# Column-tile key-value blocks for batches 2 and 3, with the second gate difference ahead of their scalings

## The chip, the cores and the metric

The kernel runs on one core of a Trainium2 chip. The metric is the device time of one execution in microseconds (us); less is better. Most executions agree within 0.3%. Times of one comparison come from the same chip and the same rounds.

## The reference, cut to what matters

```python
# attention without a score matrix, 8 batches, 8 heads, 576 tokens, 64 per head
q_s = softmax(q, axis=-1)                    # over the 64 of a head
k_s = softmax(k, axis=2)                     # over the tokens
kv  = einsum('bhsd,bhse->bhde', k_s, v)      # a 64x64 matrix per head
x   = einsum('bhsd,bhde->bhse', q_s, kv)     # -> (4608, 512)
# then a two-layer network
h = x @ w_in                                 # 512 -> 2048
g = h / (1 + exp(-beta * h))
out = g @ w_out                              # 2048 -> 512
```

## The kernel before

The work goes in nine slabs of 512 tokens. In slab t, TensorE makes the hidden tiles (`XT,WIN` matmuls, L387), ScalarE applies the gate, VectorE scales, and then (from slab 1 on) an output stage runs 112 gate products (L754) by a seven-product scheme that needs sums and differences of the gate halves. Attention for the next batches is fitted into the output stage. All engines run their own instructions in the order in which the program lists them. `tick` counts TensorE's progress; a pair `(99, f)` means that f is listed when the count reaches 99.

What the change touches:

```python
def tiled(b):
    return b > 3

# key-value products, one pair of heads: full 128-column matmul, or two
# 64-column matmuls side by side on two column tiles
if not tiled(b):
    mm(PS[bk][:, 256*n:256*n + VW-1], l, r_[:, 0:VW-1], j == 0, j == 4, ...)
for h in range(2) if tiled(b) else ():
    e.matmul(PS[bk][64*h:64*h+64, ...D+1], l[:, p], r_[:, HW*h:HW*h+D+1],
             tile_position=(0, 64*h), ...)
# when a pair of head pairs is done, VectorE scales it into weights ("scaling")
e.reciprocal(RC...)                           # L461
kvd(b, h2, bk, 256*m)                         # L433: KVD <- PS, RC, MASK
...
def g_diff(fh):                               # gate difference, L720, VectorE
    # GT[half] -= GT[other half], 128x2048 bf16, both inputs in SBUF

def norm_turn(b, hp0):                        # queries of two head pairs
    norm_main(b, hp0, 2, POOL)                # sums on VectorE, scaling on GpSimd (L343)
    turn(b, hp0, 2)                           # transpose by DMA: QT <- EQ

def attn_late(b):
    ...                                       # x: the four query products QT,KVD
    if b < 4:
        s = spread(kv_steps(b, (0, 1)), 97, 101) + spread(kv_steps(b, (2, 3)), 101, 105)
        s += [(105, lambda: g_diff(1))]
        return s + spread(x[0:2], 117, 120)
    s = [(96, steps(kv_all, b)), (99, lambda: g_diff(1))]
    return s + spread(x, 107, 123)
...
# slabs 1 and 2, output stage
on(2, norm_turn, 2, 0)
on(3, norm_turn, 2, 2)
on(3, g_diff, 0)
```

A query product has the scaled keys (KVD) as weights and the transposed queries (QT) as data, so it needs both.

The softmax here doesn't subtract the row's maximum and nothing guards it: scores larger than these inputs give would overflow.

Of the kernel before, what the change touches and what calls it, by code (L numbers as in the profile page):

```python
# [42 lines left out]
class Program:  # L43
# [12 lines left out]
    def add(self, eng, fn, r=(), w=(), bank=(), slot=None, after=(), war=False):  # L56
        op = Op(eng, fn, slot)
        op.pos = len(self.ops)
        deps = op.deps
        deps.extend(after)  # L60
        for k in r:
            deps.extend(self.writer.get(k, ()))
            self.readers.setdefault(k, []).append(op)
        for k in w:
            for d in self.readers.get(k, ()):
                if d is not op and (war or not self._same(d, op)):
                    deps.append(d)
            for d in self.writer.get(k, ()):
                if not self._same(d, op):
                    deps.append(d)  # L70
            self.readers[k] = []
            self.writer[k] = [op]
        for k in bank:
            t = self.touch.setdefault(k, {})
            for e, d in t.items():
                if e != eng:
                    deps.append(d)
            t[eng] = op
        if eng == POOL and slot is None:
            if self.pool is not None:  # L80
                deps.append(self.pool)
            self.pool = op
        self.ops.append(op)
        return op
# [71 lines left out]
def bass_efficient_attn_shen__then__act_swish_beta_kernel(  # L156
# [12 lines left out]
    with ExitStack() as es:  # L169
# [209 lines left out]
        def bank(pool=MB):  # L379
            rot[0] += 1  # L380
            return pool[rot[0] % len(pool)]

        def mm(o, l, r_, start, stop, r=(), w=(), bk=0, tr=False):
            if tr:
                add(PE, lambda e: e.transpose(o, l, r_), r=r, w=w, bank=[bk])
            else:
                add(PE, lambda e: e.matmul(o, l, r_, start=start, stop=stop), r=r, w=w, bank=[bk])  # L387
# [22 lines left out]
        def kv_rows(b, hp, j):  # L410
            i = b % 2
            pi = (b // 2) % 2
            if j < 4:
                return (bass.AP(EK[i], hp * 512 + j * 128, [[2048, 128], [1, 128]]),
                        VB[i][:, j, hp, :], [("ek", i, hp)], [("vb", i, hp)], [("vone", i)])
            if b < 2:
                return (bass.AP(EKS[b], hp * 128, [[512, 128], [1, 128]]), VRS[b][:, hp, :],
                        [EKSK[b]], [("vrs", b)],
                        [("vrs0", b), ("vrsone", b, 0), ("vrsone", b, 1)])
            return (bass.AP(EKR[pi], hp * 128, [[512, 128], [1, 128]]),  # L420
                    VR[pi][b % 2][:, hp, :], [("ekr", pi, 0), ("ekr", pi, 1)],
                    [("vr", pi, b % 2)], [("vr0", pi, b % 2), ("vrone", pi, b % 2)])
# [2 lines left out]
            return b if b < 2 else 2 + b % 4  # L425

        def tiled(b):
            return b > 3

        def kvd(b, hp, bk, c):  # L430
            i = b % 2
            a = bass.AP(PS[bk], c, [[512, 128], [0 if tiled(b) else HW, 2], [1, D]])
            add(DVE, lambda e: e.scalar_tensor_tensor(  # L433
                KVD[kd(b)][:, hp, :].rearrange("p (a b) -> p a b", b=D), a, RC[i][:, hp:hp + 1],
                MASK[:, :].rearrange("p (a b) -> p a b", b=D), ALU.mult, ALU.mult),
                r=[("ps", bk), ("rc", i, hp), "mask0", "mask1", "mask2"], w=[("kvd", kd(b), hp)],
                bank=[bk])

        def kv_steps(b, hps, pool=MB):
            i = b % 2  # L440
            st = {}

            def one(n, hp, j):
                if n == 0 and j == 0:
                    st["b"] = bank(pool)
                bk = st["b"]
                l, r_, ke, kv, ko = kv_rows(b, hp, j)
                if not tiled(b):
                    mm(PS[bk][:, 256 * n:256 * n + VW - 1], l, r_[:, 0:VW - 1], j == 0, j == 4,
                       r=ke + kv, w=[("ps", bk)], bk=bk)  # L450
                for h in range(2) if tiled(b) else ():
                    p = slice(64 * h, 64 * h + 64)
                    add(PE, lambda e, h=h, p=p: e.matmul(  # L453
                        PS[bk][p, 256 * n:256 * n + D + 1], l[:, p], r_[:, HW * h:HW * h + D + 1],
                        start=j == 0, stop=j == 4, tile_position=(0, 64 * h),
                        skip_group_check=True),
                        r=ke + kv, w=[("ps", bk)], bank=[bk])
                if n == len(hps) - 1 and j == 4:
                    c, k_ = hps[0], len(hps)
                    s_ = bass.AP(PS[bk], D, [[512, 128], [256, k_]])  # L460
                    add(DVE, lambda e: e.reciprocal(RC[i][:, c:c + k_], s_),  # L461
                        r=[("ps", bk)], w=[("rc", i, h2) for h2 in hps], bank=[bk])
                    for m, h2 in enumerate(hps):
                        kvd(b, h2, bk, 256 * m)
            return [lambda n=n, hp=hp, j=j: one(n, hp, j) for n, hp in enumerate(hps)
                    for j in range(5)]
# [6 lines left out]
        def out_step(b, hp, pool=MB, eng=DVE):  # L473
            i = b % 2

            def one():
                bk = bank(pool)
                out_mm(b, hp, bk)
                add(eng, lambda e: (e.copy if eng == ACTE else e.tensor_copy)(  # L479
                    XT[i][:, hp, :], PS[bk][:, :]),  # L480
                    r=[("ps", bk)], w=[("xt", i, hp)], bank=[bk])
            return [one]
# [43 lines left out]
        def steps(fn, *a):  # L526
            return lambda: go(fn(*a))
# [12 lines left out]
        def attn_late(b):  # L540
            x = []
            for hp in range(NHP):
                x += out_step(b, hp, MB, ACTE if hp % 2 else DVE)
            if b < 4:
                s = spread(kv_steps(b, (0, 1)), 97, 101) + spread(kv_steps(b, (2, 3)), 101, 105)
                s += [(105, lambda: g_diff(1))]
                return s + spread(x[0:2], 117, 120)
            s = [(96, steps(kv_all, b)), (99, lambda: g_diff(1))]
            return s + spread(x, 107, 123)

        def spread(steps, lo, hi):
            return [(lo + (hi - lo) * k / len(steps), s) for k, s in enumerate(steps)]
# [8 lines left out]
        def go(steps):  # L561
            for s in steps:
                s()
# [137 lines left out]
        def gv(f, th, n):  # L701
            return GT[:, f:f + n, 256 * th:256 * th + 256]

        def gk(f, th, n):
            return [("gt", f + x, th) for x in range(n)]
# [12 lines left out]
        def g_diff(fh):  # L718
            f, th = NG * fh, 1 - fh
            add(DVE, lambda e: e.tensor_tensor(gv(f, th, NG), gv(f, th, NG), gv(f, 1 - th, NG),  # L720
                                               ALU.subtract),
                r=gk(f, 0, NG) + gk(f, 1, NG), w=gk(f, th, NG), war=True)
# [140 lines left out]
        for t in range(NSLAB):  # L863
# [135 lines left out]
            elif t + 2 < B:  # L999
                b = t + 2  # L1000
# [46 lines left out]
```

## Time and profile before

| | before |
|---|---|
| time, median of 3 runs | 273.48 us |
| span in the profile | 271.7 us |
| TensorE busy | 97% |
| VectorE busy | 71% |

The page gives the share of each engine and "the chain that ended last", which follows the end of the program back through what released each step. The timeline lists instructions as start, duration, engine, line, operation, output and inputs. DVE is VectorE, ACT ScalarE, POOL GpSimd, PE TensorE's matmuls and PEld its weight loads.

### The profile page before, as it was taken

To read this page: it belongs to the slowest core of one execution; us is meant where nothing else is said; L and a number is where in the kernel's file an instruction comes from. 1 tells how busy PE (TensorE), PEld (TensorE's weight loads), DVE (VectorE), ACT (ScalarE), POOL (GpSimd) and SP (SyncE) were. 2 spreads that over 40 slices of the span, in tenths; PEclk is the share of its full clock that TensorE was granted. 3 is DMA by queue.
4 is the path that set the end of the run, shared out by engine and by line. 5 is a ranking of instruction groups with operands and counts; after the bars stand their busy time and mean duration, and the time that the engine had idled before them with its cause. 6 is when DMAs were issued, how large, how long until landed. Compare 5 with 4: busy or idle time off the path is not lost.

```text
span 271.7 us, 4811 instructions
## 1 busy us (share of the span) xinstructions
PE 263.8 (97%) x1882; PEld 165.7 (61%) x1905; DVE 194.0 (71%) x416; ACT 181.0 (67%) x284; POOL 64.1 (24%) x80
## 2 busy tenths in 40 slices
PE   8899999999999999999999999999999999999994
PEld 3444444448844885478646865687458745874683
DVE  4964586887867799878786977787687548626762
ACT  4898558789287956897778847893883387018610
POOL 2790010006530089000910870037000100000000
PEclk9999999999999999999999999999999999999999
DMA  7999999989799129930499999203800130012005
GB/s 220 314 201 207 227 321 349 303 227 373 173 337 285 65 53 299 332 95 2 89 282 283 308 345 182 103 20 65 208 0 2 31 142 2 0 69 88 0 5 152
DMA packets 59366, 45.93 MB, mean 169 GB/s; under 512 B 28608, under 2 KB 58320, under 8 KB 58320
## 3 DMA queue, kind: packets, MB, share of 16 engines
q1 hardware_dynamic: 54480, 40.90, 53.4%
q0 software_dynamic: 4240, 4.19, 9.4%
q10 hardware_dynamic: 624, 0.53, 0.6%
q8 instruction: 15, 0.25, 0.4%
q14 instruction: 7, 0.06, 0.1%
HBM read 36.71 MB, written 9.44 MB: 170 GB/s over the span
## 4 chain that ended last, share of the span: by engine, by line
PE 85%; DVE 4%; DMA 4%; POOL 2%; SPq 2%; issue 2%; ACT 1%; POOLq 0%
PE PS L387 51%; PE PS L754 33%; DMA VF<-in_v_dram 2%; DMA QT<-EQ 1%; PE PS L453 1%; POOL VB L358 1%; SPq L275 1%; DVE QS L339 1%; SPq L287 1%; DVE EQ L343 1%; POOL EQ L343 1%; DVE VB L358 1%; ACT GT L654 1%; POOL VR L372 0%; DVE QI L341 0%
## 5 line engine op out<-in xcount | busy, mean ns | idle before, releaser
L387 PE MATMUL PS<-XT,WIN 128*128 128x512 bf16 x562 | 126.2, 379 | 1.1 <-issue 0.3
L654 ACT ACTIVATE GT<-PS,BETA 128x512 bf16<-128x512 f32 x144 | 95.1, 689 | 37.8 <-PE PS L387 37.5
L387 PEld LDWEIGHTS PS<-XT,WIN 128*128 128x128 bf16 x576 | 55.2, 98 | 64.4 <-DVE XT L479 0.6
L677 DVE TENSOR_SCALAR GT<-GT,RB 128x512 bf16<-128x512 bf16 x144 | 52.1, 382 | 36.5 <-ACT GT L654 35.6
L343 POOL TENSOR_TENSOR EQ<-EQ,QI 128x1024 bf16<-128x1024 bf16 (+1 forms) x13 | 25.6, 1967 | 46.9 <-DVE QI L341 46.3
L754 PE MATMUL PS<-WOUT,GT 128*128 128x256 bf16 x256 | 33.0, 273 | 0.1
L754 PE MATMUL PS<-WOUT,GS 128*128 128x256 bf16 x256 | 31.9, 273 | 0.2
L754 PE MATMUL PS<-WSUM,GT 128*128 128x256 bf16 x256 | 30.4, 273 | 0.5 <-DMA QT<-EQ 0.4
L754 PEld LDWEIGHTS PS<-WSUM,GT 128*128 128x128 bf16 x256 | 25.0, 98 | 3.8 <-issue 0.3
L754 PEld LDWEIGHTS PS<-WOUT,GT 128*128 128x128 bf16 x256 | 24.9, 98 | 3.5
L790 ACT COPY O2S<-PS 128x512 f32<-128x512 f32 (+1 forms) x17 | 9.4, 560 | 25.6 <-PE PS L754 24.2
L754 PEld LDWEIGHTS PS<-WOUT,GS 128*128 128x128 bf16 x256 | 24.1, 98 | 3.4
L307 ACT ACTIVATE EQ<-QF 128x512 bf16<-128x512 f32 x32 | 17.9, 620 | 7.3 <-DMA QF<-in_q_dram 7.2
L358 POOL CAST VB<-VF 128x512 bf16<-128x512 f32 x24 | 16.7, 694 | 23.0 <-DVE GS L713 14.1
L713 DVE TENSOR_TENSOR GS<-GT 128x512 bf16<-128x512 bf16 (+2 forms) x32 | 21.9, 685 | 0.0
L339 DVE TENSOR_REDUCE QS<-EQ 128x16 f32<-128x1024 bf16 (+1 forms) x20 | 19.8, 991 | 0.9 <-ACT EQ L307 0.9
L720 DVE TENSOR_TENSOR GT<-GT 128x2048 bf16<-128x2048 bf16 x16 | 20.1, 1281 | 0.0
L307 ACT ACTIVATE EK<-KF 128x512 bf16<-128x512 f32 x32 | 18.1, 620 | 0.1
L479 ACT CAST XT<-PS 128x512 bf16<-128x512 f32 x18 | 10.3, 581 | 10.7 <-PE PS L387 10.7
L802 DVE TENSOR_TENSOR O2S<-TS,PS 128x512 f32<-128x512 f32 (+1 forms) x17 | 10.7, 643 | 9.5 <-PE PS L754 9.5
L754 PE MATMUL PS<-WSUM,GS 128*128 128x256 bf16 x128 | 16.7, 273 | 0.0
L387 PE MATMUL PS<-WOUT,GT 128*128 128x512 bf16 x62 | 15.0, 379 | 0.1
(82 smaller groups left out, 225.5 us busy)
## 6 DMA issues: line engine op xcount, KB each, us to landing
out_dram<-O2S SPq DMA_DIRECT2D x8, 1024.0 KB, 5.4
QF<-in_q_dram SPq DMA_DIRECT2D x6, 1024.0 KB, 5.9
KF<-in_k_dram SPq DMA_DIRECT2D x6, 1024.0 KB, 8.5
VF<-in_v_dram SPq DMA_DIRECT2D x6, 1024.0 KB, 12.2
KF<-in_k_dram SPq DMA_DIRECT2D x8, 256.0 KB, 5.5
VF<-in_v_dram SPq DMA_DIRECT2D x8, 256.0 KB, 5.5
WOUT<-in_moe_w_out_dram POOLq DMA_DIRECT2D x4, 512.0 KB, 16.4
WIN<-in_moe_w_in_dram POOLq DMA_DIRECT2D x3, 512.0 KB, 9.0
```

Source lines behind the costliest of these rows:

```text
L307: add(ACTE, lambda e, o=o, a=a: e.activation(o, a, ACT.Exp), r=[(name + "f", i, hp)], w=[("e" + name, i, hp)])
L339: add(DVE, lambda e: e.tensor_reduce(s_, a, AX.X, ALU.add), r=ks, w=[("qs", i, hp0)])
L343: add(eng, lambda e: e.tensor_tensor(a, a, vb, ALU.mult), r=ks + [("qi", i, hp0)], w=ks)
L358: add(eng, lambda e: (e.copy if eng == ACTE else e.tensor_copy)(o, a), r=[("vf", i, hp), ("vone", i)], w=[("vb", i, hp)], after=after)
L387: add(PE, lambda e: e.matmul(o, l, r_, start=start, stop=stop), r=r, w=w, bank=[bk])
L479: add(eng, lambda e: (e.copy if eng == ACTE else e.tensor_copy)(XT[i][:, hp, :], PS[bk][:, :]), r=[("ps", bk)], w=[("xt", i, hp)], bank=[bk])
L654: add(ACTE, lambda e: e.activation(GT[:, f, :], PS[bk][:, :], ACT.Silu, scale=BETA[:, f:f + 1]), r=[("ps", bk), "beta"], w=[("gt", f, 0), ...
L677: add(DVE, lambda e: e.tensor_scalar(GT[:, f, :], GT[:, f, :], RB[:, f:f + 1], None, ALU.mult), r=k + ["rb"], w=k)
L713: add(DVE, lambda e: e.tensor_tensor(GS2[:, i:i + n, :], GT[:, i:i + n, :], GT[:, i + NG:i + NG + n, :], ALU.add), r=[k_ for f in (i, i + ...
L720: add(DVE, lambda e: e.tensor_tensor(gv(f, th, NG), gv(f, th, NG), gv(f, 1 - th, NG), ALU.subtract), r=gk(f, 0, NG) + gk(f, 1, NG), w=gk(f ...
L754: add(PE, lambda e, l=l, r_=r_, st=st, u=u, i=i, b_=b_: e.matmul(PS[b_][:, 256 * u:256 * u + 256], l, r_, start=st, stop=end and i == NG - ...
L802: add(DVE, lambda e, b_=b_, u0=u0, u1=u1: e.tensor_tensor(o[:, u0:u1, :], ts[:, u0:u1, :], bank3(b_)[:, u0:u1, :], ALU.add), r=["ts", ("ps ...
```

## The change

The intent: batches 4 to 7 already have their key-value products as blocks on column tiles, which take TensorE less time (0.84 us for a batch, measured in slab 3, against an estimated 1.13); batches 2 and 3 get them too. With the block in one piece, the second gate difference is put ahead of the block in the program, and so ahead of its scalings on VectorE.

```diff
         def tiled(b):
-            return b > 3
+            return b > 1
...
             if b < 4:
-                s = spread(kv_steps(b, (0, 1)), 97, 101) + spread(kv_steps(b, (2, 3)), 101, 105)
-                s += [(105, lambda: g_diff(1))]
+                s = [(99, lambda: g_diff(1)), (101, steps(kv_all, b))]
                 return s + spread(x[0:2], 117, 120)
```

## The prediction

> **What bounds the kernel now.** I read first the page's busy shares and the chain that ended last, then the timeline of the two places that the change touches, then the waits there, then a later stage for the rule that decides.
>
> ```profile
> PE 263.8 (97%) x1882; PEld 165.7 (61%) x1905; DVE 194.0 (71%) x416; ACT 181.0 (67%) x284; POOL 64.1 (24%) x80
> ...
> PE 85%; DVE 4%; DMA 4%; POOL 2%; SPq 2%; issue 2%; ACT 1%; POOLq 0%
> ```
>
> TensorE carries 85% of the chain. A TensorE saving therefore counts, unless TensorE runs into a wait right behind it. The change touches only the output stages of slabs 1 and 2 (the key-value products of batches 2 and 3), so I look there. The chain in order of time, slab 1:
>
> ```profile
> 66.96 1.91 POOL EQ L343
> 68.86 0.02 issue
> 68.88 3.53 DMA QT<-EQ
> 72.41 0.27 issue
> 72.68 0.49 PE PS L754 x3
> ```
>
> Here TensorE does not set the time. The query scaling on GpSimd and its transpose DMA do: TensorE stands before the first query product until 72.45, when the transpose lands. The timelines of VectorE, then of GpSimd, at that place (start, duration):
>
> ```profile
> 68.68 1.26 DVE L720 TENSOR_TENSOR GT<-GT 128x2048 bf16<-128x2048 bf16 x1
> 69.86 0.16 DVE L461 RECIPROCAL RC<-PS 128x2 f32<-128x2 f32 x1
> 70.05 0.61 DVE L433 SCALAR_TENSOR_TENSOR KVD<-PS,RC,MASK 128x128 bf16<-128x128 f32 x2
> 70.58 0.16 DVE L461 RECIPROCAL RC<-PS 128x2 f32<-128x2 f32 x1
> 70.77 0.61 DVE L433 SCALAR_TENSOR_TENSOR KVD<-PS,RC,MASK 128x128 bf16<-128x128 f32 x2
> 71.30 1.48 DVE L720 TENSOR_TENSOR GT<-GT 128x2048 bf16<-128x2048 bf16 x1
> 72.88 0.69 DVE L479 CAST XT<-PS 128x512 bf16<-128x512 f32 x1
> ```
> ```profile
> 68.94 2.76 POOL L343 TENSOR_TENSOR EQ<-EQ,QI 128x1024 bf16<-128x1024 bf16 x1
> ```
>
> L720 is a gate difference, L461 and L433 are the key-value scalings. GpSimd's second query scaling takes 2.76 us beside the first gate difference, its twin just before took 1.91. And the second gate difference, begun at 71.30, ends 1.08 us after GpSimd's end at 71.70. In slab 2 the same rows stand at 97.25 (first difference), 97.50 (GpSimd, 2.76) and 99.86 (second difference, end 101.34). The waits from 94 to 106 us, slab 2:
>
> ```profile
> PEld PS L387 <- DMA QT<-EQ: 0.5, 2, 0.3
> PEld PS L754 <- issue: 0.3, 1, 0.3
> ```
>
> The two QT waits are for the first and the second transpose. The "issue" one ends at 101.46, just after the second gate difference: it is the wait for it.
>
> **What the Trainium skill says.** "SBUF — State Buffer", section "Who interferes with whom": VectorE and GpSimd share a port pair, an exclusive lock for the whole instruction; a VectorE operation with two SBUF inputs contends with a GpSimd operation that reads SBUF. The trace agrees: gate differences are such operations, and the 2.76 and 1.48 above are these locks. "VectorE: DVE Perf Modes", section "The perf-mode tier table", gives 1224 ns for a bf16 tensor_tensor of 2048 elements; the undisturbed ones in this trace take 1218 ns. "TensorEngine Tiling (Array Packing)", section "Key Properties", says that changing the tiling mode drains TensorE; the gap of some 0.1 us at the end of the tiled block below agrees. "TensorE: Matmul & The Clock Gate", section "What's actually happening", puts the idle window before a slower clock at some 3.4 us; no wait here shows it, and the ones that I predict are shorter.
>
> What happens when VectorE issues two contending instructions in a row while GpSimd waits? Slab 4 shows it:
>
> ```profile
> 152.91 2.77 DVE L720 TENSOR_TENSOR GT<-GT 128x2048 bf16<-128x2048 bf16 x2
> 152.94 1.66 POOL L358 CAST VB<-VF 128x512 bf16<-128x512 f32 x1
> ...
> 154.04 1.63 DVE L720 TENSOR_TENSOR GT<-GT 128x2048 bf16<-128x2048 bf16 x1
> ```
>
> The cast (0.61 us when alone) waits out the first difference, which ends at 154.12, and ends at 154.60; the second difference, issued at 154.04, then takes until 155.67, 1.07 us after the cast. So they alternate: the waiting GpSimd goes in between the two.
>
> **The change part by part.**
>
> (a) TensorE. Per batch, 20 full matmuls of 131 columns, strewn among gate products, become 40 matmuls of 65 columns in one block, pairs side by side on two column tiles. Before: from one gate product to the next takes 0.11 us, with a key-value matmul between 0.167, so about 0.057 each and 20 x 0.057 = 1.13 us. After, from batch 4 in slab 3, already tiled: the block begins at 123.80 (0.11 after the gate product before it at 123.69), the next gate product at 124.64: 0.84 us. Saved: 0.29 us per batch. The block also starts 7 gate products later (0.76 us), so the wait for the key exponentials (0.22 us at 67.69, slab 1) vanishes. TensorE reaches the first query product of slab 1 some 0.5 us earlier, of slab 2 0.3 us earlier. But it waits there already for the transpose, which the change does not speed up: all of this is lost in a longer wait.
>
> (b) VectorE. No work is removed. The order first difference, scalings, second difference becomes first difference, second difference, scalings. By the alternation of slab 4 the second difference, though issued at 69.86 in slab 1, waits until GpSimd ends at 71.70 and ends at 72.77: the very time at which it ended before. GpSimd and the transposes do not move. What moves is the four scalings. They ran in the shadow of the GpSimd operation (69.86 to 71.38); they now begin after 72.77. From the end of a gate difference (69.93) to the end of the first scaling (70.40) took 0.47 us, to the last (71.38) 1.45 us. So the first scaling ends at 72.77 + 0.47 = 73.24 in slab 1 and 101.34 + 0.47 = 101.81 in slab 2.
>
> (c) The path. The first query product has the scaled keys as weights. From VectorE's end to TensorE's start I take 0.12 us (second difference end 101.34, weights at 101.46).
> Slab 1: 73.36 instead of 72.45: +0.91. Behind it, the next query product needs the second scaling at 73.50, and arrives there at 73.8; the second transpose landed by 74.97 and is wanted at 75.9; the cast of the first query output goes from 73.88 at most to 74.8, wanted at 75.9. No further wait: +0.91 stays.
> Slab 2: 101.93 instead of 100.58: +1.35. The wait for the second difference is gone; in matmul starts it cost 101.49 - 101.36 = 0.14. The wait for the second transpose (103.53 against 103.45 without it: 0.08) goes too, as TensorE now comes later than the landing. The last query output's cast on VectorE, pushed by 1.25, would end at 106.56, wanted at 106.8. Net 1.35 - 0.14 - 0.08 = +1.13.
>
> Sum: 0.91 + 1.13 = +2.0 us. From 104 us on the chain is TensorE alone with waits of 0.05, so nothing absorbs the shift. 273.48 + 2.0 = 275.5; I take off 0.1 for small slack: 275.4.
>
> **The rivals.**
> 1. VectorE keeps the lock for both differences. Then the second ends at about 71.0, the scalings are ready at 71.5, before the transpose, and the first product waits as before. But GpSimd ends 1.1 us later (72.8), and so the second transpose: 1.0 us of new wait at 74.97, and about 1.1 at 103.53. Total about +2.1: nearly the same time by another wait. Slab 4 speaks against it.
> 2. Nothing contends, and the TensorE saving reaches the end: 0.5 + 0.3, and the 0.14 for the second difference: about 272.6. Against it: the transposes, which set 72.45, 100.58 and 103.53, do not come earlier.
> 3. The saving is hidden and the scalings come in time (the second difference gets the port at once and GpSimd is not hurt): 273.5. Against it: GpSimd's 2.76.
> 4. The longer TensorE pauses (in slab 1 from 72.45 - 0.46 - 0.5 = 71.5 to 73.4: 1.9 us) lower its clock: some us more. The clock row shows 9 throughout, with no pause this long, so it can't be excluded from this trace.
>
> **Range and chances.** Two ways of arbitration both give +2.0 to +2.1; what is open is the size of latencies (some 0.2 per slab) and whether VectorE's backlog costs slab 2 a little more. 8 in 10: 274.4 to 276.1. Two per cent is 5.5 us, more than any reckoning here gives; only a fallen clock could do it. Faster by over 2%: 0.005; within: 0.985; slower: 0.01.
>
> **What would show it.** In the changed profile: the key-value group of 128x131 over EKR gone, 80 more matmuls of 65 columns, blocks near 0.84 us (step a). On VectorE, in slabs 1 and 2, the second difference about 2.9 us long, ending where it ended before, with scalings after it; GpSimd's second scaling still about 2.76 (step b). If that one is near 3.8 and the second difference 1.2, rival 1 holds. Among the waits, TensorE on the scalings (L433) in slabs 1 and 2, about 1.9 us long each, in place of QT (step c). A time under 273.2 would say that the transposes no longer hold TensorE; above 276.5, that VectorE's backlog or the clock costs more than I saw.

## More of the kernel before

To compare kernels I cut the span at the first combining step of each output stage on VectorE (`TS<-PS`, COPY): "stage 1" runs from that of slab 1 to that of slab 2, "stage 2" to that of slab 3. This is the table of the kernel before by such stretches (from:to, length, then busy time and count for each engine, then clock):

```profile
63.90:92.47 28.57, 28.12 (x200) 18.64 (x201) 21.79 (x43) 20.25 (x32) 9.72 (x11) 1.00 0.86 257
92.47:120.83 28.36, 28.18 (x200) 18.54 (x201) 24.66 (x47) 21.71 (x35) 12.94 (x10) 1.00 0.65 187
120.83:149.57 28.74, 28.48 (x264) 19.00 (x266) 22.43 (x51) 22.77 (x38) 7.33 (x7) 1.00 0.61 156
```

Stages 1 and 2 hold everything that the change moves.

## The result

| | before | after |
|---|---|---|
| time, median of 6 runs | 273.45 us | 275.57 us |
| lowest to highest | 273.27 to 273.69 | 275.36 to 276.28 |
| ratio | | 1.008 (95%: 1.0067 to 1.0093) |

A ratio here is the mean time of one kernel's runs over the mean of the other's runs of the same rounds, so it is not quite the ratio of the medians quoted beside it. The changed kernel is slower by 0.8%.

The same stretches in the changed kernel:

```profile
63.58:93.07 29.49, 27.66 (x220) 18.18 (x221) 23.16 (x44) 20.27 (x33) 9.75 (x11) 1.00 0.88 258
93.07:122.56 29.49, 27.66 (x220) 18.17 (x221) 25.50 (x48) 21.72 (x36) 13.05 (x10) 1.00 0.69 179
122.56:151.29 28.73, 28.46 (x264) 18.96 (x266) 22.43 (x51) 22.78 (x38) 7.34 (x7) 1.00 0.58 151
```

TensorE's busy time fell in both stages (28.12 to 27.66, 28.18 to 27.66), and yet the stages grew: by 29.49 - 28.57 = 0.92 and 29.49 - 28.36 = 1.13 us. The third is the same to 0.01. So the loss lies wholly in these two stages, and it is waiting, not work. (The two profiles differ by 1.7 us in span and not by 2.05, because the stretch ahead of stage 1 was 0.32 us shorter in this execution. It varied between 63.5 and 64.3 over all profiles, whatever the kernel. That is why the stages are read from the profile and the total from the timed runs.)

Slab 1 on VectorE and GpSimd after, to be held against the same rows shown in the prediction:

```profile
69.53 2.92 DVE L719 TENSOR_TENSOR GT<-GT 128x2048 bf16<-128x2048 bf16 x1
72.38 0.16 DVE L461 RECIPROCAL RC<-PS 128x2 f32<-128x2 f32 x1
72.57 0.61 DVE L433 SCALAR_TENSOR_TENSOR KVD<-PS,RC,MASK 128x128 bf16<-128x128 f32 x2
```
```profile
68.61 2.76 POOL L343 TENSOR_TENSOR EQ<-EQ,QI 128x1024 bf16<-128x1024 bf16 x1
```

The second difference (now L719) is issued at once, takes 2.92 us in place of 1.48, and ends 1.08 us after GpSimd's end at 71.37. The GpSimd instruction keeps its 2.76. Both differences together last from 68.35 to 72.45, 4.10 us; before, from 68.68 to 72.78, also 4.10, but then the four scalings lay inside that time. Now they lie behind it.

The chain in order of time at this place (start, length, what) changed its owner:

```profile
68.44 4.01 DVE GT L719 x2
72.45 0.09 DVE RC L461
...
72.57 0.61 DVE KVD L433 x2
...
73.28 0.49 PE PS L753 x3
```

Before, the GpSimd scaling and the transpose stood here. Now the two gate differences and the scalings do. The waits of this stretch name it less clearly:

```profile
PEld PS L387 <- DMA QT<-EQ: 1.8, 1, 1.8
PE PS L753 <- DVE RC L461: 1.8, 1, 1.8
```

The first query product's weight load waited 1.8 us, and the view says "QT", one of the two things that it needs. But the transpose landed 3.9 us after its issue at 68.56, that is at 72.49, while the first scaling ended at 72.92 and the load began at 73.03. The later one decided. In slab 2 the load's wait is called "issue" by the profile.

### The profile page after: what moved, and what is told of

Read it like the earlier page. It is cut to its first block, busy times and chain, and to the rows that moved or that the text cites. A ratio compares the mean times of both kernels' runs of the same rounds, so it can differ in the third digit from the quotient of the medians.

```text
span 273.4 us, 4889 instructions
## 1 busy us (share of the span) xinstructions
PE 262.4 (96%) x1922; PEld 164.7 (60%) x1945; DVE 196.2 (72%) x416; ACT 181.0 (66%) x284; POOL 64.5 (24%) x80
## 4 chain that ended last, share of the span: by engine, by line
PE 83%; DVE 11%; DMA 2%; SPq 2%; issue 1%; ACT 0%; DVEq 0%
PE PS L387 50%; PE PS L753 31%; DVE GT L719 3%; DVE QS L339 3%; DMA VF<-in_v_dram 2%; PE PS L453 1%; SPq L275 1%; SPq L287 1%; DVE EQ L343 1%; DVE QI L341 1%; DVE KVD L433 1%; DVE VB L358 1%; DVE TS L822 1%; DVE TS L825 1%; DVE TS L831 0%
## 5 line engine op out<-in xcount | busy, mean ns | idle before, releaser
L676 DVE TENSOR_SCALAR GT<-GT,RB 128x512 bf16<-128x512 bf16 x144 | 51.5, 377 | 37.1 <-ACT GT L653 36.5
L753 PE MATMUL PS<-WOUT,GT 128*128 128x256 bf16 x256 | 30.9, 273 | 0.1
L719 DVE TENSOR_TENSOR GT<-GT 128x2048 bf16<-128x2048 bf16 x16 | 22.8, 1462 | 0.0
```

The lines of the kernel that those rows point to most:

```text
L676: add(DVE, lambda e: e.tensor_scalar(GT[:, f, :], GT[:, f, :], RB[:, f:f + 1], None, ALU.mult), r=k + ["rb"], w=k)
L719: add(DVE, lambda e: e.tensor_tensor(gv(f, th, NG), gv(f, th, NG), gv(f, 1 - th, NG), ALU.subtract), r=gk(f, 0, NG) + gk(f, 1, NG), w=gk(f ...
L753: add(PE, lambda e, l=l, r_=r_, st=st, u=u, i=i, b_=b_: e.matmul(PS[b_][:, 256 * u:256 * u + 256], l, r_, start=st, stop=end and i == NG - ...
```

## The experiments

Two parts were changed at once, so each was tried alone; then the suspected cause, GpSimd's lock, was taken away, halved and turned round; then the readings were used to look for a better kernel. All results were correct except where a wrong one is announced.

**1. The blocks alone.** From the changed kernel:

```diff
-                s = [(99, lambda: g_diff(1)), (101, steps(kv_all, b))]
+                s = [(101, steps(kv_all, b)), (105, lambda: g_diff(1))]
```

> The 65-column blocks alone, VectorE's order as before (first difference, scalings, second difference). My theory (GpSimd's scaling and its transposes, not TensorE, set the end of slabs 1 and 2): TensorE arrives 0.5 and 0.3 us earlier at the first query product and waits that much longer; 273.45 us within 0.2. Rival (the TensorE saving reaches the end): 272.7. Rival (blocks on column tiles cost TensorE time): above 274.

Measured: 274.02 us against 273.71 for the kernel before, ratio 1.0015 (0.9999 to 1.003). Stage 1 took 28.89 us (28.57 before), stage 2 28.33 (28.36). TensorE's timeline in slab 1 (the last field is the idle time ahead and what ended it):

```profile
72.84 0.39 PE L387 MATMUL PS<-QT,KVD 128*128 128x512 bf16 x1 [0.95 <-DMA QT<-EQ]
```

TensorE arrived earlier and waited 0.95 us for the transpose. The saved time does not reach the end. The 0.32 us more in stage 1 come from the transpose, which was issued at the same place (0.20 us after the start of the first difference in both) and landed 3.9 us later here, 3.5 in the profile of before. It took between 3.1 and 4.5 over the runs. So the blocks neither gain nor cost anything that I can tell from this variation. The time is 0.31 us above the kernel before, more than the 0.2 that I allowed, and by the number alone it touches the last of the three guesses (a cost of the blocks, above 274). Against that guess stands stage 2, where the first transpose took 3.1 us in both profiles: 28.33 us with the blocks, 28.36 without.

**2. The order alone.** From the kernel before:

```diff
-                s += [(105, lambda: g_diff(1))]
+                s += [(96.9, lambda: g_diff(1))]
```

> Full key-value matmuls strewn as before, only the second gate difference moved ahead of the scalings. My theory: the whole loss is here, 275.5 us (+2.0, within 0.3): second difference about 2.9 us long, first query product held until the first scaling, some 0.9 us later in slab 1 and 1.3 in slab 2. Rival (the loss comes from the block, its mode switch or its late start): 273.5 or less.

Measured: 275.83 us against 273.71, ratio 1.0083 (1.0069 to 1.0097): the whole loss. Stages 29.57 and 29.49. Slab 2 of this run, VectorE and then TensorE:

```profile
99.43 2.92 DVE L720 TENSOR_TENSOR GT<-GT 128x2048 bf16<-128x2048 bf16 x1
102.27 0.16 DVE L461 RECIPROCAL RC<-PS 128x2 f32<-128x2 f32 x1
102.46 0.61 DVE L433 SCALAR_TENSOR_TENSOR KVD<-PS,RC,MASK 128x128 bf16<-128x128 f32 x2
```
```profile
102.96 0.38 PE L387 MATMUL PS<-QT,KVD 128*128 128x512 bf16 x1 [1.27 <-DVE KVD L433]
```

Here the profile names the scaling itself as what TensorE waited for. In slab 1 of this one profile the transpose happened to land late (4.5 us after issue), about when the first scaling was ready, so that slab alone would not have told the two apart.

**3. GpSimd's second query scaling taken out,** in batches 2 and 3, from the changed kernel and from the kernel before (both give a wrong result):

```diff
-            norm_main(b, hp0, 2, POOL)
+            norm_main(b, hp0, 2, POOL, mult=not (hp0 == 2 and b in (2, 3)))
```

> The changed kernel without GpSimd's second query scaling in batches 2 and 3 (a wrong result on purpose). If that instruction's lock is the cause, the second difference takes 1.2 us, the scalings come before the transpose lands, and all of the loss is gone: 273.2 us, the same within 0.3 as the kernel before with the same cut. If the order on VectorE costs by itself, or the blocks do, it stays a good part of 2 us above that.

> The control: the kernel before with the same cut (a wrong result on purpose). My theory: it loses only the waits for the second difference (0.14) and the second transpose (0.08) of slab 2: 273.2 us.

Measured: changed kernel with the cut 273.61 us, kernel before with the cut 273.63, uncut kernel before in the same rounds 273.50; ratios to that 1.0005 (0.999 to 1.002) and 1.0012 (0.9995 to 1.0029). The two differences in the cut changed kernel:

```profile
68.70 2.39 DVE L719 TENSOR_TENSOR GT<-GT 128x2048 bf16<-128x2048 bf16 x2
```

2.39 us for both, in place of 4.10. With the GpSimd instruction gone the order on VectorE costs nothing. So the order is harmful only together with that instruction. The control's small gain of 0.3 us that I expected was not to be seen in the times; it is about the size of the run-to-run variation. In the profiles, one of each, it does show: the control's stages are 28.48 and 28.13 us, 0.32 less in all than those of the uncut kernel. The cut changed kernel has 28.85 and 28.19; its first transpose in stage 1 landed 3.81 us after issue, the control's 3.44, which is the 0.37 between them.

**4. The same GpSimd work in two halves.** The scaling and its transpose of batches 2 and 3 are cut per head pair, from the changed kernel:

```diff
+            if hp0 == 2 and b in (2, 3):
+                norm_main(b, 2, 2, mult=False)           # sums as before
+                for hp in (2, 3):
+                    add(POOL, ... tensor_tensor(a, a, vb, ALU.mult) ...)  # 128x512
+                    turn(b, hp, 1)
+                return
```

> The changed kernel, with GpSimd's second query scaling and its transpose cut into two halves in batches 2 and 3. If waiting engines alternate on the shared port, the second difference gets in after one half: it is some 2.0 us long in place of 2.9, the first scaling ends 0.9 us earlier, and the loss falls from 2.0 to about 0.6 us: 274.0 us. If the lock were held by GpSimd across its queued instructions, the second difference stays at 2.9 or longer and the time at 275.5.

Measured: 274.03 us against 273.71, ratio 1.0016 (1.0004 to 1.0028), stages 28.67 and 28.63. The second difference and the first half:

```profile
70.20 2.06 DVE L729 TENSOR_TENSOR GT<-GT 128x2048 bf16<-128x2048 bf16 x1
```
```profile
69.28 1.90 POOL L522 TENSOR_TENSOR EQ<-EQ,QI 128x512 bf16<-128x512 bf16 x1
```

The difference takes 2.06 us in place of 2.92: it gets in after the first half (end 71.18) and ends 1.08 later. Then the second half waits in its turn. This agrees with taking turns, and excludes that GpSimd keeps VectorE out over its whole queue. (Taking turns and being served in order of issue come to the same in all these runs: the half had been issued at 69.28, before the difference, and the second half only at 71.26, after it.) Halving the instruction gave back about four fifths of the loss.

**5. GpSimd made to wait for the second difference,** the arrangement of the prediction's first rival: the scaling is listed behind the difference and depends on it; the loads of the next batches are kept behind its transpose.

```diff
-                s = [(99, lambda: g_diff(1)), (101, steps(kv_all, b))]
+                s = [(99, lambda: g_diff(1)), (99.1, lambda: mult_turn(b)),
+                     (101, steps(kv_all, b))]
```

> The changed kernel with GpSimd's second query scaling made to wait for the second difference: the arrangement of the prediction's first rival. Second difference 1.2 us long, no wait for the scalings, but the scaling on GpSimd ends 1.1 us later and so does the second transpose: waits of about 1.0 and 1.1 us for the second transpose at the start of slabs 2 and 3. Time 275.5 us, within 0.4: the same loss by another wait.

Measured: 277.87 us against 273.50, ratio 1.0162 (1.0126 to 1.0198): a loss of the expected kind but twice the expected size. The two differences took 2.39 us, as expected. The waits view puts 0.5 and 0.4 us of waiting down to the scalings, but by the end times the first transpose decided there (first scaling done at 71.62 and 101.36, landing at 72.16 and 101.81), again as expected; and the waits for the second transpose came. Stages 1 and 2 took 29.74 and 32.07 us. Their size was off for two reasons. First, GpSimd began 0.15 us after the difference's end and then took its full 1.90, where I had reckoned 1.76 from that end; and the transpose of slab 2 landed 3.80 us after its issue. Second, after the wait at the start of slab 3 this happened (TensorE's timeline, then the table by stretches):

```profile
106.81 0.39 PE L387 MATMUL PS<-QT,KVD 128*128 128x512 bf16 x1 [2.06 <-DMA QT<-EQ]
...
107.69 4.65 PE L387 MATMUL PS<-XT,WIN 128*128 128x512 bf16 x13
```
```profile
104.00:108.00 4.00, 1.94 (x11) 0.88 (x10) 1.56 (x4) 0.74 (x2) 3.60 (x6) 0.96 0.89 217
108.00:112.00 4.00, 4.00 (x13) 1.48 (x12) 2.36 (x4) 2.20 (x3) 2.98 (x2) 0.61 1.08 361
```

The third number from the right is TensorE's granted clock: 0.61 between 108 and 112. The record has it at half from 107.68 for 3.4 us, which by my estimate costs half of that, some 1.7. The four runs fall into two pairs, as the clock does: 276.85 and 277.10 us with a mean clock of 0.998 and 1.0, 278.64 and 278.86 with 0.994. The clock fell in half of the runs.

**6. Looking for a better kernel.** Halved scalings let the second difference end early; if the query products came later, TensorE could go on with gate products meanwhile. First try, on experiment 4:

```diff
-                return s + spread(x[0:2], 117, 120)
+                return s + spread(x[0:2], 121, 124)
...
-todo += [..., (2.5, steps(out_step, t, 3))]
+todo += [..., (4.5, steps(out_step, t, 3))]
```

> As split2, with the first two query products of batches 2 and 3 placed 4 ticks later, behind 4 and 7 of the last gate products, and the fourth one 2 ticks later. The second difference is now done early enough that TensorE runs on into these gate products while the transpose is still under way. My theory: slab 1 gains 0.7 and slab 2 some 0.5 us against the kernel before: 272.2 us. If the transposes bind all the same: 274 or more.

Measured: 274.97 us, ratio 1.005 (1.0035 to 1.0064), worse than expected by far. Stage 1 fell to 28.32, stage 2 rose to 29.76. The waits of slab 2:

```profile
PEld PS L387 <- DVE XT L479: 2.3, 2, 1.8
```

The later query product is also listed later on VectorE: its output's cast now stood behind a reduction of 1.2 us for another batch. I had moved one engine's instruction and forgotten that this moves the other engine's. Four further steps, each mending what the profile of the one before showed (from here on the second scaling is halved and two scalings stand on either side of the second difference):

> split2_late mended where its profile showed waits: in batches 2 and 3 both early query outputs are evacuated by ScalarE (on VectorE the first stood behind a reduction), two scalings stand ahead of the second difference and two behind it, and the fourth query product is 0.6 ticks earlier. My theory: TensorE gains 0.7 and 0.45 us up to the next slab's first products, but the second half of the second transpose, now later, takes most of it back: 273.2 us, 0.3 below the kernel before. If something else held split2_late back: 274 or more.

> split3, and the first products of slabs 2 and 3 run over four tiles in place of three before the third query output is needed (0.4 us more time for the transpose, 0.65 for the last output). If the late transpose is what took the gain back, 272.4 us, 1.1 below the kernel before; if not, as split3.

> The control for split4: the same later query products, four tiles and ScalarE evacuations, but GpSimd's scaling whole and all scalings ahead of the second difference as in the kernel before. The second difference then ends as late as before and TensorE waits for it in place of the transpose: no gain, 273.9 us within 0.4. If the gain of split4 comes from the later products alone, this one gains too.

> split4 with the fifth tile of slabs 2 and 3 put into a PSUM bank that the output stage has just left (split4's profile shows TensorE waiting 0.5 us there for ScalarE's first activation, as four tiles in the lead leave no free bank). If that wait is what ate split4's gain, the two stages fall to 28.3 and 27.8 us (28.57 and 28.36 before): 272.7 us, 0.8 below the kernel before. If the wait only moves one tile on, 273.5.

> split5 with the first key-value block 1.9 ticks later, as the changed kernel has it nearly: in split5's profile TensorE waits 0.3 us before that block for ScalarE's key exponentials of batch 2. Stage 1 falls from 28.48 to 28.2 us, stage 2 stays at 28.0: 273.0 us, 0.7 below the kernel before. If the last query output on VectorE or a transpose takes the 0.3 us back, 273.3.

| kernel | edit | us | before, same rounds | ratio (95%) | stages 1, 2 |
|---|---|---|---|---|---|
| split2_late: halves, later products | see above | 274.97 | 273.71 | 1.005 (1.0035 to 1.0064) | 28.32, 29.76 |
| split3: + casts on ScalarE, split order | `ACTE if hp % 2 or (b < 4 and hp == 0) else DVE` | 273.52 | 273.77 | 0.9999 (0.9985 to 1.0012) | 28.48, 28.02 |
| split4: + four tiles in the lead | `nl = 4 if t in (2, 3) else 3` | 273.84 | 273.77 | 1.0007 (0.9993 to 1.0021) | 28.79, 28.30 |
| late4_whole: the same, scaling whole (control) | halves undone, all scalings ahead of the second difference | 274.82 | 273.77 | 1.0043 (1.0029 to 1.0057) | 29.00, 29.00 |
| split5: + fifth tile in a free bank | `3 if n == 3 else 4 if n == nl else None` | 273.31 | 273.71 | 0.998 (0.9956 to 1.0004) | 28.48, 27.99 |
| split6: + first key-value block later | `(98.9, steps(kv_steps, b, (0, 1)))` for 97 | 273.17 | 273.67 | 0.9985 (0.997 to 0.9999) | 28.04, 27.99 |

The expectations of split4 (272.4 us) and split5 (272.7) were missed by 1.4 and 0.6 us. The four tiles used up the banks of PSUM, the memory that the matmuls write to. The waits of split4 between 70 and 82 us show TensorE held by ScalarE's first activation:

```profile
PEld PS L387 <- ACT GT L664: 0.6, 1, 0.6
```

The fifth tile in another bank removed that wait, and stage 2 fell by 0.3; the later key-value block removed a wait of 0.3 us for key exponentials. The control shows that the later products alone gain nothing: with the scaling whole, TensorE waits for the second difference instead (and for the same PSUM bank), and the kernel is 1.0 us slower than its twin with halves. (The twin also has two scalings behind the second difference, so the 1.0 us is not shown to be the halves' alone.) In the last kernel the second difference in slab 2 is nearly free of waiting:

```profile
99.02 1.34 DVE L730 TENSOR_TENSOR GT<-GT 128x2048 bf16<-128x2048 bf16 x1
```

It is the only version below both kernels whose interval excludes 1, and only just, as the last of five variants tried: 0.15% by the ratio, 0.5 us by the medians. Its two stages together are 56.93 - 56.03 = 0.90 us shorter than those of before in one profile each. The timed gain is smaller than that, and its size stays open within the variation.

## Why the prediction was right

The time was 275.57 us, forecast 275.4 with 274.4 to 276.1. What matters is whether it came out by its own steps.

*Step a, TensorE.* Right. The block of slab 1 ran from 67.42 (0.11 after the gate product before it) to 68.27, 0.85 us where 0.84 was taken from batch 4. In slab 2 the stretch of 32 gate products that holds the key-value products, up to the first product with weight sums (`WSUM,GT`), went from 4.64 us (94.46 to 99.10) to 4.36 (95.05 to 99.41): 0.28 saved, 0.29 forecast. (The busy time of the stages fell by more, but the ends of matmuls are modelled, so I go by their starts.) Experiment 1 shows that the saving ends in a longer wait for the transpose.

*Step b, VectorE.* Right in each number: the second difference 2.92 us long (2.9 forecast), its end at an unchanged distance from the start of the first, GpSimd at 2.76, the scalings behind. That GpSimd's second scaling is the cause is shown by experiments 3 and 4, not only argued: without the instruction the loss is gone, cut in two it costs a fifth. That the two engines meet at a shared port is the account that the prediction cites; the durations fit it, but no run here tells a port from another resource that both would take in turns.

*Step c, the path.* Right: +0.92 and +1.13 us against +0.91 and +1.13. That slab 1 agrees to 0.01 us is partly luck: before, its length follows a transpose that landed after 3.5 us in the one profile that I read, and after 3.1 to 4.5 over this study. The sum before my deduction was 275.5; the deduction of 0.1 "for small slack" had no ground, as the later stages are the same to 0.01 us. I expected the waits view to name the scalings. It named the transpose and a reciprocal in slab 1, "issue" and the same reciprocal in slab 2, and only the chain and the end times settled it.

*The rivals.* The first does not occur by itself. The forecast that it would come to "nearly the same time by another wait" was wrong: made to occur (by a dependency, not by a lock kept), it cost 3.35 and 3.6 us in the runs without a fallen clock and over 5 in the others, where I had 2.1. The step that failed there is the size of GpSimd's delay and of the transpose's landing. The fourth rival, a falling clock, did not happen in the changed kernel, with a pause of 1.78 us and a clock of 1.00 in both stages; in experiment 5 it did, after a pause of 2.06.

## What to carry to other kernels

Before you move an instruction ahead of others on its engine, ask what it will wait for in its new place: work that ran in the shadow of a wait is pushed out of it when the waiting instruction goes first. A faster engine gains nothing where it already waits for something else, so look at what ends the wait behind the saving before you count the saving. Where two engines take turns, cutting the long instruction in two gives the other a place to get in.

## What the Trainium skill lacked or had wrong

- "SBUF — State Buffer", section "Who interferes with whom", says that whoever issues first gets the shared pair for the whole instruction. It gives no case in which one engine has two such instructions in a row. Here the first of the two gave no claim to the second, and every one went in order of issue: of two differences issued back to back, the second came after the waiting GpSimd instruction (2.92 us long), after half of it when that was halved (2.06 us), and at once when it was gone (2.39 us for both).
- "TensorE: Matmul & The Clock Gate", section "What's actually happening", puts the fall to half clock after at least one idle window of some 3.4 us. It does not say how idle such a window has to be. In experiment 5 the clock was halved for 3.4 us although TensorE had been busy for 1.34 of the 3.41 us before, with one pause of 2.06 us between matmuls (one run's trace; the mean clock of two of its four runs points to the same). Pauses of 1.78 us, in the changed kernel, did not do it in the one profile taken.
- No page that I read gives the time of a single DMA transpose from issue to landing or its variation: the first transpose of batch 2 took 3.1 to 4.5 us over the profiles here, and this sets stage 1 wherever the scalings are done in time.
